# Groups of 384 tokens for the last two batches of the first product, and retimed start-up work, in a memory-attention kernel with two MLPs

## The chip, the core and the metric

The kernel runs on one core of a Trainium2 chip. The metric is the device time of one execution in microseconds. Three runs of the kernel before took 741.64 to 742.65 us, median 742.09. The engines are PE (TensorE, matmuls), PEld (its weight loads, which run beside matmuls), DVE (VectorE), ACT (ScalarE), POOL (GpSimd) and SP (SyncE, which here only issues DMAs).

## The reference

There are 4 batches, 8 heads, 576 tokens a batch, heads of 64 and 32 memory slots a head. `phi` gives a softmax over tokens, with which k and v are summed into 32 memory rows; q attends to these rows. The result, 2304 tokens of 512 features, goes through two MLPs of 512 x 2048 x 512, the first with a leaky ReLU, the second with the Mish function. All arithmetic is float32; the MLPs' weights come as 64-bit floats.

```python
a = exp(phi - max over tokens); a = a / (sum over tokens + 1e-9)
k_m = einsum('bhsm,bhsd->bhmd', a, k)
v_m = einsum('bhsm,bhsd->bhmd', a, v)
attn = softmax(q @ k_m.T / 8)               # over the 32 slots
x = (attn @ v_m), heads side by side        # 2304 x 512
h = x @ w_in;   x = max(0.01 * h, h) @ w_out
h = x @ w_in2;  out = (h * tanh(softplus(h))) @ w_out2
```

## The kernel before

**Numbers.** A float32 factor is split into a high part (a copy rounded to the matmul type fp32r) and a low part (the factor minus the high part). A product takes three matmuls: high weights by high data, low weights by high data, high weights by low data. `hi_lo` (L317) makes the two parts: the copy on ACT or DVE, the subtraction on DVE. The weights come as 64-bit floats and are decoded as two 32-bit words (`decode`, L359): ACT scales the high word (L369), the low word is shifted down to its top three bits on ACT (L374) or DVE (L376), DVE joins them (L411).

**Stage 1** is attention and the first MLP. The memory rows of v are multiplied into `w_in` first (`vw_tasks`, L955, matmuls of L975): for each batch and each chunk c of 512 of the 2048 hidden features there are two weight tiles `vw` (one for each group of four heads) of 2 x 512 words, high and low. There are eight buffers of that kind (`vw_tag`), taken in turn. `at` holds the attention weights, high and low, of 576 tokens; there are four such buffers, two a batch.

One item (`stage1`, L1215) is a block m of 128 hidden features for half a batch, 288 tokens. Its h product has 6 matmuls of 128x128 by 128x288 (L1226) into one of two PSUM tiles. ACT applies the leaky ReLU twice, into the high tile and into a plain one (L1240); DVE subtracts them into the low tile (L1247). Two items later (`LAG1`) come 8 matmuls of high parts and 4 of the low part with `w_out` (L1259) into four PSUM accumulators, one for each 128 output features. After the last block the accumulators are copied or added to `x1` (L1304 and L312). Batches 0 and 1 go in turns of one or two chunks while weights still arrive; batches 2 and 3 go through all 16 blocks, first for one half and then for the other.

**Stage 2** is the second MLP with Strassen's seven products at 384 columns (L1579, L1791; 256 columns at the end). Its data factors come from `split_x` (L1477), which needs the space of the attention buffers: all users of the pool `apool` must be through (`apool_users`, `keep`). Its weight factors (`split_w`, L1416) lie in the buffers that `w_out` and `vw` leave (`slots`, L1335). `w_in2` and `w_out2` are prepared during stage 1 (from L1113), partly in views of the attention's `kvq` buffers.

**Order.** Nothing waits by hand. Each piece of work is a task with a cost on each engine that can do it, a priority, tasks it depends on and buffers it takes. `Order.run` (L94) plays them through with those costs when the kernel is built: at each time an idle engine gets the ready task with the lowest priority, on the engine that would end it first, plus a bias (`TOP` for the low-word shift on DVE, `HI` for copies on DVE). A task that takes a buffer may start at most 8 items ahead. The order that comes out is fixed in the program of each engine; on the chip semaphores keep the dependences. Priorities count in items: `A1` and `A2` say how many items before a batch's first its attention is due, `S1` and `S2` how far apart its halves are, `WO` and `WC` how long before its item a block of w_out or a chunk of w_in is due, `V0` to `V2` the same for vw, `PL` and `BH` when and behind which chunk-1 loads of w_in the second batch's loads are issued on SP's queue, `HFD` the spacing of the steps of batch 0's attention, `XL` how long before the end of stage 1 the splits of x are due.

Of the kernel before, what the change touches and what calls it, by code (L numbers as in the profile page):

```python
# [23 lines left out]
def hop(a, b):  # L24
# [4 lines left out]


K = dict(
    LAG1=2, WIN=8, OB=2, RS=4, FILL=58, A1=10, S1=8.0,
    A2=30, S2=2.6, V1=2.4, V2=14, W2=45, W2S=3.8, O='phi0 kv0 phi1 q0 w0 kv1 q1 w1 w2 w3', HF0=-20.0, HF1=-7.0,
    HFD=0.3, TOP=0.1, HI=0.2, WO=2.0, WOL=1, WC=3.0, WC0=-38.0, V0=3.0, COLD=20, GL=1.5, AL=5.0, XL=22.0, T='0:1 0:1 1:2 0:2 1:2', SB=1,
    DW=280e3, DQ=1.3, DP=1.2, DS=0.78, DI=0.38, L4=0.5, L4P=1.6, L4S=0.8, L4T=5.0, MA=6, QL=4, PL=6, BH=(9,3,3,3,3), FK=-52.5, DWF=0.85, MV="......rvvrrvvrvr",
)


# [121 lines left out]
def kernel(  # L160
# [12 lines left out]
    nc = tc.nc  # L173
# [778 lines left out]

    win, win_ready, w_scr, w_loads = {}, {}, {}, [[] for _ in range(NC)]

    def vw_tasks(b, c, p0):  # L955
# [26 lines left out]

        t = keep(add(
            {"PE": 1.2}, p0, f, [x for g in range(NG) for x in vT[b, g][1] + win_ready[b, c, g]],
            pss + us, [vT[b, g][0] for g in range(NG)] + wbs,
        ))
        for g in range(NG):
            u, ps_b = us[g], pss[g]
            th, tl = hi_lo(
                p0 + 0.5 * g + 0.2, 512, lambda u=u: u.t[:, 0], lambda u=u: u.t[:, 1], lambda ps_b=ps_b: ps_b.t,  # L990
                [t], (), [u, ps_b], ps=True,
            )
            vw[b, c, g] = (u, th, tl)


# [12 lines left out]
    n1 = len(items)  # L1008
    at_item = {it: i for i, it in enumerate(items)}
    base = [at_item["1", b, 0, 0] for b in range(B)]  # L1010


    def wo_unit(m):
# [52 lines left out]
    def next_batch(b):  # L1066
        d, st = (K["A1"], K["S1"]) if b == 1 else (K["A2"], K["S2"])
        p = base[b] - d
        kv_rest(b, p, 0.08 * d / 2)
        score_rest(b, p + 0.1 * d, (p + 0.3 * d, p + 0.3 * d + st), 0.03 * d)  # L1070

    def next_vw(b, c):
        vw_tasks(b, c, at_item["1", b, 0, 4 * c] - (K["V1"] if b == 1 else K["V2"]))

    for b, cs in chunk_turns:
        if b and not cs[0]:
            next_batch(b)
        for c in cs:
            if b:
                next_vw(b, c)  # L1080
                continue
            w_chunk(c)
            for m in range(4 * c, 4 * c + 4):
                wo_unit(m)


    kv_again = [kvq.new([P, 2, 1024]) for _ in range(2)]
    opened = [add({"SP": 0.0}, K["W2"], lambda e, x=x: x.make(), (), [x]) for x in kv_again]

    class View:  # L1090

# [14 lines left out]
            b.make = make  # L1106
            return b

    views = [View(j) for j in range(3)]
# [102 lines left out]
    def passes(n):  # L1212
        return [(j, wi) for j in range(n) for wi in range(2)]

    def stage1(i, b, sub, m):  # L1215
        cols = slice(sub * NB1, (sub + 1) * NB1)
        c, j0 = m // 4, (m % 4) * P
        h = h_tag.new([P, NB1])
        us, ats = [vw[b, c, g] for g in range(NG)], [at[b, g] for g in range(NG)]

        def f1(e):
            h.make()
            n = 0
            for g in range(NG):
                for wi, ai in ((0, 0), (1, 0), (0, 1)):
                    nc.tensor.matmul(  # L1226
                        out=h.t, lhsT=us[g][0].t[:, wi, j0:j0 + P], rhs=ats[g][0].t[:, ai, cols],
                        start=(n == 0), stop=(n == 3 * NG - 1),
                    )
                    n += 1  # L1230

        t1 = add(
            {"PE": mm(NB1, 6)}, i, f1, [x for u in us for x in u[1:]] + [x for u in ats for x in u[1 + sub]], [h],
            [u[0] for u in us + ats],
        )
        t1.main = i
        eb, hb, lb = e_tag.new([P, NB1]), hi_tag.new([P, NB1], F32R), lo_tag.new([P, NB1], F32R)

        def lrelu(o):
            nc.scalar.activation(out=o, in_=h.t, func=AF.Prelu, alpha=0.01)  # L1240


        t4 = add({"ACT": act(NB1, True)}, i + 0.3, lambda e: lrelu(hb.make()), [t1], [hb], [h])
        t3 = add({"ACT": act(NB1, True)}, i + 0.4, lambda e: lrelu(eb.make()), [t1, t4], [eb], [h])
        t5 = add(
            {"DVE": dve(NB1)}, i + 0.6,
            lambda e: nc.vector.tensor_tensor(out=lb.make(), in0=eb.t, in1=hb.t.bitcast(F32), op=ALU.subtract),  # L1247
            [t4, t3], [lb], [eb, hb],
        )
        first, last = m in firsts(b), m + 1 in firsts(b) + [NM]  # L1250
        if first:
            for kk in range(NK):
                accs[kk] = acc_tag.new([P, NB1])
        ac = dict(accs)
        wu = wo[m]

# [11 lines left out]
        if first:  # L1268
            for kk in range(NK):
# [1 line left out]
                    ac[kk].make()  # L1271
                    mms([(kk, 0, 0), (kk, 1, 0)])

                hs.append(add({"PE": mm(NB1, 2)}, i + LAG1 + 0.01 * kk, f, [t4, *wu[1:], *hs[-1:]], [ac[kk]], [hb, wu[0]]))
        else:
            hs.append(
                add(
                    {"PE": mm(NB1, 2 * NK)}, i + LAG1, lambda e: mms([(kk, wi, 0) for kk, wi in passes(NK)]),
                    [t4, *wu[1:], *prev_l], (), [hb, wu[0], *ac.values()],
                )  # L1280
            )
# [1 line left out]
        if last:  # L1283
            for kk in range(NK):
                tl = add(
                    {"PE": mm(NB1)}, i + LAG1 + 0.1 + 0.01 * kk, lambda e, kk=kk: mms([(kk, 0, 1)]),
                    [t5, *hs], (), [lb, wu[0], ac[kk]],
                )
                key = (b, kk // 2)
                fresh = key not in x1  # L1290
                if fresh:
                    if b < B - 1:
                        x1[key] = [x1_tag.new([P, 2, S]), {}]
                    else:
                        x1[key] = [at_tag.new([P, 2, S]), {}]
                xb, evs = x1[key]
                add_in = (kk, sub) in evs

                def fe(e, kk=kk, xb=xb, fresh=fresh, add_in=add_in):
                    if fresh:  # L1300
                        xb.make()
                    o = xb.t[:, kk % 2, cols]
                    if add_in:
                        nc.vector.tensor_tensor(out=o, in0=ac[kk].t, in1=o, op=ALU.add)  # L1304
                    else:
                        copy(e, o, ac[kk].t)

                deps = [tl] + [x for x in list(evs.values())[:1]]
                if add_in:
                    deps.append(evs[kk, sub])  # L1310
                evs[kk, sub] = add(
                    {"DVE": dve(NB1)} if add_in else {"ACT": act(NB1, True), "DVE": dve(NB1)},
                    i + LAG1 + 0.2, fe, deps, [xb] if fresh else [], [ac[kk]] if fresh else [ac[kk], xb],
                )
        else:
            tl = add(
                {"PE": mm(NB1, NK)}, i + LAG1 + 0.1, lambda e: mms([(kk, 0, 1) for kk in range(NK)]),
                [t5, *hs], (), [lb, wu[0], *ac.values()],
            )
            prev_l.append(tl)  # L1320

    prev_l = []
    for i in range(n1):
        stage1(i, *items[i][1:])

# [566 lines left out]
```

## Time and profile before

| | us |
|---|---|
| median of 3 runs | 742.09 (741.64 to 742.65) |
| the profiled execution | 741.87 |
| its span, first to last instruction | 740.1 |
| PE busy in it | 731.0 |
| PEld busy | 701.3 |
| DVE busy | 550.6 |
| ACT busy | 402.5 |

The profile is of one execution. The span leaves out 1.8 us of the execution's own time. A busy PE is one with a matmul in flight; matmuls overlap, so the mean length of one (297 ns for 288 columns) is not the distance from one to the next. PEld's weight loads run beside the matmuls. The granted TensorE clock is 0.999 on the mean.

### The profile page before, as it was taken

To read this page: it belongs to the slowest core of one execution; us is meant where nothing else is said; L and a number is where in the kernel's file an instruction comes from. 1 tells how busy PE (TensorE), PEld (TensorE's weight loads), DVE (VectorE), ACT (ScalarE), POOL (GpSimd) and SP (SyncE) were. 2 spreads that over 40 slices of the span, in tenths; PEclk is the share of its full clock that TensorE was granted. 3 is DMA by queue.
4 is the path that set the end of the run, shared out by engine and by line. 5 is a ranking of instruction groups with operands and counts; after the bars stand their busy time and mean duration, and the time that the engine had idled before them with its cause. 6 is when DMAs were issued, how large, how long until landed. Compare 5 with 4: busy or idle time off the path is not lost.

```text
span 740.1 us, 15587 instructions
## 1 busy us (share of the span) xinstructions
PE 731.0 (99%) x5875; PEld 701.3 (95%) x5875; DVE 550.6 (74%) x1153; ACT 402.5 (54%) x877; POOL 0.7 (0%) x6
## 2 busy tenths in 40 slices
PE   8999999999999999999999999999999999999997
PEld 7788899888999989999999999999999999999997
DVE  6899868598766965647859797867777966775595
ACT  4866458565553775645546665544464644444442
POOL 0000000000000000000000000000000000000000
PEclk9999999999999999999999999999999999999999
DMA  9793957787869587863559898788988778996475
GB/s 353 299 318 115 350 172 232 229 274 229 290 207 286 171 274 269 262 233 101 199 199 338 302 312 254 233 271 249 300 278 264 250 239 258 297 290 207 126 218 182
DMA packets 99322, 183.73 MB, mean 248 GB/s; under 512 B 8112, under 2 KB 51376, under 8 KB 99248
## 3 DMA queue, kind: packets, MB, share of 16 engines
q1 hardware_dynamic: 99248, 182.75, 75.5%
q8 instruction: 46, 0.75, 0.4%
q14 instruction: 28, 0.23, 0.1%
HBM read 140.25 MB, written 42.47 MB: 247 GB/s over the span
## 4 chain that ended last, share of the span: by engine, by line
PE 96%; DVE 2%; ACT 1%; DMA 0%; issue 0%
PE acc_t L1259 28%; PE h_t L1579 22%; PE acc_t L1791 22%; PE h_t L1226 13%; PE misc_t L1791 2%; PE misc_t L975 2%; PE acc_t L1579 2%; PE acc_t L508 1%; PE misc_t L741 1%; PE misc_t L646 1%; DMA phi_t<-in_phi_dram 0%; PE h_t L865 0%; ACT raws_t L369 0%; ACT raws_t L374 0%; PE misc_t L689 0%
## 5 line engine op out<-in xcount | busy, mean ns | idle before, releaser
L1259 PE MATMUL acc_t<-hi_t,wo_t 128*128 128x288 f32 x1024 | 160.6, 297 | 0.4 <-DVE x_t L312 0.3
L1259 PEld LDWEIGHTS acc_t<-hi_t,wo_t 128*128 128x128 f32 x1024 | 142.9, 188 | 12.2 <-issue 7.0
L1226 PE MATMUL h_t<-at_t,vw_t 128*128 128x288 f32 x768 | 123.1, 296 | 0.0
L1791 PE MATMUL acc_t<-hi_t,wo_t 128*128 128x384 f32 x448 | 114.4, 336 | 0.0
L1240 ACT ACTIVATE hi_t<-h_t 128x288 fp32r<-128x288 f32 x128 | 52.6, 411 | 111.8 <-PE acc_t L1259 105.3
L1226 PEld LDWEIGHTS h_t<-at_t,vw_t 128*128 128x128 f32 x768 | 108.5, 188 | 0.7 <-issue 0.6
L1247 DVE TENSOR_TENSOR lo_t<-e_t,hi_t 128x288 fp32r<-128x288 f32 x128 | 57.3, 450 | 47.4 <-ACT e_t L1240 21.6
L1259 PE MATMUL acc_t<-lo_t,wo_t 128*128 128x288 f32 x512 | 89.8, 297 | 0.5 <-DVE lo_t L1247 0.5
L1791 PEld LDWEIGHTS acc_t<-hi_t,wo_t 128*128 128x128 f32 x448 | 81.3, 188 | 0.0
L1259 PEld LDWEIGHTS acc_t<-lo_t,wo_t 128*128 128x128 f32 x512 | 74.7, 188 | 6.3 <-issue 5.6
L1579 PE MATMUL h_t<-xt_t,vw_t 128*128 128x384 f32 x396 | 79.4, 336 | 0.0
L1579 PE MATMUL h_t<-xt_t,wo_t 128*128 128x384 f32 x352 | 75.8, 336 | 0.0
L1791 PE MATMUL acc_t<-lo_t,wo_t 128*128 128x384 f32 x224 | 75.6, 337 | 0.0
L1758 DVE TENSOR_TENSOR lo_t<-wo_t,hi_t 128x384 fp32r<-128x384 f32 x94 | 52.0, 554 | 31.4 <-ACT hi_t L310 29.9
L1579 PEld LDWEIGHTS h_t<-xt_t,vw_t 128*128 128x128 f32 x396 | 69.3, 188 | 0.0
L310 ACT ACTIVATE hi_t<-wo_t 128x384 fp32r<-128x384 f32 x78 | 40.7, 524 | 40.7 <-PE acc_t L1791 36.4
L1579 PEld LDWEIGHTS h_t<-xt_t,wo_t 128*128 128x128 f32 x352 | 61.9, 188 | 0.0
L1240 ACT ACTIVATE e_t<-h_t 128x288 f32<-128x288 f32 x128 | 52.0, 406 | 0.0
L1791 PE MATMUL acc_t<-wo_t,hi_t 128*128 128x256 f32 x240 | 45.0, 282 | 0.0
L1604 ACT ACTIVATE wo_t<-wo_t 128x384 f32<-128x384 f32 x53 | 27.6, 522 | 30.8 <-DVE wo_t L1598 30.6
L1791 PEld LDWEIGHTS acc_t<-lo_t,wo_t 128*128 128x128 f32 x224 | 42.0, 188 | 0.0
L310 ACT ACTIVATE wo_t<-h_t 128x384 f32<-128x384 f32 x50 | 24.5, 489 | 31.1 <-PE h_t L1579 31.1
(263 smaller groups left out, 1110.0 us busy)
## 6 DMA issues: line engine op xcount, KB each, us to landing
wo_t<-tscr SPq DMA_DIRECT2D x168, 256.0 KB, 3.8
vw_t<-wsum SPq DMA_DIRECT2D x32, 512.0 KB, 4.7
win_t<-wscr SPq DMA_DIRECT2D x24, 512.0 KB, 5.5
raw_t<-in_moe_w_in_dram SPq DMA_DIRECT2D x19, 512.0 KB, 7.5
raw_t<-in_moe_w_out_dram SPq DMA_DIRECT2D x17, 512.0 KB, 5.5
wsum<-vw_t SPq DMA_DIRECT2D x16, 512.0 KB, 4.5
wo_t<-wsum SPq DMA_DIRECT2D x16, 512.0 KB, 4.3
tscr<-raw_t SPq DMA_DIRECT2D x9, 512.0 KB, 5.5
```

What stands on the lines that cost most here:

```text
L310: nc.scalar.activation(out=o, in_=i, func=AF.Copy)
L508: nc.tensor.matmul(out=acc.t[rows, :].rearrange("p (j d) -> p j d", j=2), lhsT=phv()[rows, r, :], rhs=kv.t[rows, :2304].rearrange("p (j r ...
L646: nc.tensor.matmul(out=accs_[g].t[o:o + M, :].rearrange("p (j d) -> p j d", j=2), lhsT=ph.t[rows, x, j, :], rhs=kv[g].t[rows, :, x % 2, j, :],
L975: nc.tensor.matmul(out=pss[g].t[M * (h ^ g):M * (h ^ g) + M, :], lhsT=vT[b, g][0].t[rows, g, h ^ g if b else h // 2, :], rhs=wbs[g].t[rows ...
L1226: nc.tensor.matmul(out=h.t, lhsT=us[g][0].t[:, wi, j0:j0 + P], rhs=ats[g][0].t[:, ai, cols], start=(n == 0), stop=(n == 3 * NG - 1),)
L1240: nc.scalar.activation(out=o, in_=h.t, func=AF.Prelu, alpha=0.01)
L1247: lambda e: nc.vector.tensor_tensor(out=lb.make(), in0=eb.t, in1=hb.t.bitcast(F32), op=ALU.subtract),
L1259: nc.tensor.matmul(out=ac[kk].t, lhsT=wu[0].t[:, wi, kk * P:(kk + 1) * P], rhs=(hb if src == 0 else lb).t, start=(first and (wi, src) == ( ...
L1579: nc.tensor.matmul(out=h.t, lhsT=w[:, wi, c0:c0 + P], rhs=xp[b, xi].ap()[:, j], start=(first and j == 0 and k3 == 0), stop=(j == 1 and k3 ...
L1604: lambda e: nc.scalar.activation(out=t_of[x](), in_=h.t if h else t_of[x](), func=AF.Mish),
L1758: lambda e, hb=hb, lb=lb, src=src: nc.vector.tensor_tensor(out=lb.make(), in0=src(), in1=hb.t.bitcast(F32), op=ALU.subtract),
L1791: nc.tensor.matmul(out=ac[t].t, lhsT=T[:, wi, t * P:(t + 1) * P] if wide else x.t[:, t * P:(t + 1) * P], rhs=x.t if wide else T[:, wi], st ...
```

## The change

The tokens of batches 2 and 3, 1152 together, are cut into three groups of 384 rather than four of 288. The first lies in batch 2, the last in batch 3, and the middle one has 192 tokens of each. For the middle group a block's h is computed in two parts, side by side in one PSUM tile, each with the vw and at tiles of its own batch; ACT, DVE and the products with w_out treat the 384 columns as one, and the accumulators are copied out in two parts.

Batch 2's eight vw tiles are then in use until the middle group is through, so batch 3's tiles of chunk 0 lie elsewhere: one in the buffer of phi, the other in the two T buffers of attention (`Two`). Both are in `apool`, so the blocks that use them count among the users that `split_x` waits for. Positions of batches 2 and 3 count in steps of 384/288 items. The opening of the `kvq` views for w_in2 and w_out2 moves up into the loop over batches.

Eleven values change. Among them: the bias against the low-word shift on DVE rises from 0.1 to 0.4, the second batch's attention is due 12 items ahead rather than 10, w_out blocks are due at their item rather than two before it, and x is due 18 items before the end of stage 1 rather than 22.

```diff
-    ... A1=10, S1=8.0,
-    A2=30, S2=2.6, ...
-    HFD=0.3, TOP=0.1, HI=0.2, WO=2.0, WOL=1, WC=3.0, WC0=-38.0, V0=3.0, COLD=20, GL=1.5, AL=5.0, XL=22.0, ...
-    ... PL=6, BH=(9,3,3,3,3), ...
+    ... A1=12, S1=8.0,
+    A2=30, S2=3.5, ...
+    HFD=0.38, TOP=0.4, HI=0.2, WO=0.0, WOL=1, WC=3.5, WC0=-38.0, V0=2.0, COLD=20, GL=2.5, AL=5.0, XL=18.0, ...
+    ... PL=5, BH=(9,3,3,2,3), ...
...
+    class Two:
+        def __init__(self, bufs):
+            self.bufs = bufs
+        def make(self):
+            for x in self.bufs:
+                x.make()
+            self.t = self
+        def __getitem__(self, key):
+            return self.bufs[key[1]].t[key[:1] + key[2:]]
...
-            us.append(vw_tag.new([P, 2, 512], F32R))
+            if b == B - 1 and not c and g:
+                us.append(Two([T_tag.new([P, 512], F32R) for _ in range(2)]))
+            else:
+                us.append((vw_tag if b < B - 1 or c else tags["phi"]).new([P, 2, 512], F32R))
...
+            if b == B - 1 and not c:
+                keep(th), keep(tl)
...
-    items = [("1", b, sub, m) for b, m0, m1 in turns for sub in range(NSUB) for m in range(m0, m1)]
+    items = [("1", b, sub, m) for b, m0, m1 in turns for sub in range(NSUB) for m in range(m0, m1) if b < 2]
+    n_pair = len(items)
+    W3 = NB2 / NB1
+    for j in range(3):
+        parts = [(2, NB2 * j, min(NB2, S - NB2 * j))] if j < 2 else []
+        if j:
+            parts.append((3, 0 if j == 1 else S - NB2, NB2 if j == 2 else 2 * NB2 - S))
+        items += [("3", j, parts, m) for m in range(NM)]
...
-    def stage1(i, b, sub, m):
+    def stage1(i, step, parts, m):
+        N, b0 = sum(n for _, _, n in parts), parts[0][0]
...
-        h = h_tag.new([P, NB1])
+        h = h_tag.new([P, N])
...
+            o = 0
+            for x, (b, c0, n) in enumerate(parts):
+                for g in range(NG):
+                    for wi, ai in ((0, 0), (1, 0), (0, 1)):
+                        nc.tensor.matmul(
+                            out=h.t[:, o:o + n], lhsT=us[NG * x + g][0].t[:, wi, j0:j0 + P], rhs=ats[NG * x + g][0].t[:, ai, c0:c0 + n],
+                            start=((g, wi, ai) == (0, 0, 0)), stop=((g, ai) == (NG - 1, 1)), skip_group_check=True,
+                        )
+                o += n
...
+        if parts[-1][0] == B - 1 and not c:
+            keep(t1)
...
+        lag = LAG1 * step
...
-    slots = [
-        (base[B - 1] + NM + x, t) for x, _, t in sorted(
-            [(LAG1 + m, 0, wo_tag) for m in range(NM)] + [(4 * c + 3, 1, vw_tag) for c in range(NC) for _ in range(2)],
+    at_end = lambda m: n_pair + W3 * (2 * NM + m)
+    slots = [
+        (x, t) for x, _, t in sorted(
+            [(at_end(LAG1 + m), 0, wo_tag) for m in range(NM)] + [(at_end(4 * c + 3 if c else 0), 1, vw_tag) for c in range(NC) for _ in range(2)],
```

## Rows read from the trace of the kernel before

**Rows 1.** The page's parts 1 and 4: busy us of each engine; the chain that ended last.

```profile
PE 731.0 (99%) x5875; PEld 701.3 (95%) x5875; DVE 550.6 (74%) x1153; ACT 402.5 (54%) x877; POOL 0.7 (0%) x6
...
PE 96%; DVE 2%; ACT 1%; DMA 0%; issue 0%
```

**Rows 2.** Windows of one shape: stretch, length, busy and count by engine, clock, DMA.

```profile
350.00:370.00 20.00, 20.00 (x153) 20.00 (x153) 17.19 (x34) 11.66 (x27) 0.00 (x0) 1.00 0.52 184
480.00:520.00 40.00, 40.00 (x231) 40.00 (x230) 27.88 (x62) 17.36 (x35) 0.00 (x0) 1.00 0.83 256
...
710.00:730.00 20.00, 20.00 (x169) 20.00 (x168) 16.72 (x38) 9.78 (x19) 0.00 (x0) 1.00 0.81 247
```

**Rows 3.** Lines by shape: count, busy us, mean ns of one, idle before.

```profile
L1259 PE MATMUL acc_t<-hi_t,wo_t 128*128 128x288 f32 x1024 | 160.6, 297 | 0.4 <-DVE x_t L312 0.3
...
L1791 PE MATMUL acc_t<-hi_t,wo_t 128*128 128x384 f32 x448 | 114.4, 336 | 0.0
L1226 PEld LDWEIGHTS h_t<-at_t,vw_t 128*128 128x128 f32 x768 | 108.5, 188 | 0.7 <-issue 0.6
...
L1791 PE MATMUL acc_t<-wo_t,hi_t 128*128 128x256 f32 x240 | 45.0, 282 | 0.0
...
L623 PEld LDWEIGHTS misc_t<-ones,rm_t 128*128 128x128 f32 x12 | 1.6, 190 | 0.1
```

**Rows 4.** Timeline, weight loads near 56.6: start, us, instruction, count.

```profile
56.59 0.52 PEld L623 LDWEIGHTS misc_t<-ones,rm_t 128*128 128x128 f32 x4
```

**Rows 5.** Timeline, the boundary between batches 2 and 3.

```profile
307.53 0.30 PEld L1259 LDWEIGHTS acc_t<-hi_t,wo_t 128*128 128x128 f32 x2 [0.39 <-DVE x_t L312]
```

**Rows 6.** Timeline, the last vw preparation of batch 3.

```profile
298.13 1.09 PE L975 MATMUL misc_t<-win_t,vTb_t 64*32 64x512 f32 x16
...
299.96 1.22 DVE L1184 TENSOR_TENSOR kvq_t<-kvq_t 128x1024 fp32r<-128x1024 f32 x1
...
301.09 1.28 DVE L326 TENSOR_TENSOR vw_t<-misc_t,vw_t 128x512 fp32r<-128x512 f32 x2
```

**Rows 7.** Timeline, splits of x on DVE and stage 2's first product.

```profile
332.67 0.56 DVE L312 CAST xt_t<-x_t 128x768 fp32r<-128x768 f32 x1
...
349.68 0.56 DVE L1539 TENSOR_TENSOR raw_t<-raw_t,x_t 128x384 f32<-128x384 f32 x1
...
374.34 1.21 PE L1579 MATMUL h_t<-xt_t,wo_t 128*128 128x384 f32 x6
```

**Rows 8.** Windows of the end of stage 1.

```profile
330.00:350.00 20.00, 20.00 (x153) 20.00 (x152) 13.61 (x27) 10.94 (x27) 0.00 (x0) 1.00 0.31 107
350.00:374.00 24.00, 24.00 (x183) 24.00 (x183) 18.53 (x36) 13.16 (x32) 0.00 (x0) 1.00 0.59 208
```

**Rows 9.** Timeline, PE and DVE in the first items.

```profile
36.68 1.27 PE L1057 MATMUL acc_t<-ident 128*128 128x128 f32 x10
...
37.54 0.68 DVE L326 TENSOR_TENSOR wo_t<-raws_t,wo_t 128x512 fp32r<-128x512 f32 x1
...
39.01 0.79 PE L1259 MATMUL acc_t<-lo_t,wo_t 128*128 128x288 f32 x4 [0.47 <-DVE lo_t L1247]
```

**Rows 10.** Lines by shape from 0 to 110 us: low-word shifts.

```profile
L374 ACT ACTIVATE raw_t<-raw_t 128x512 int32<-128x512 uint16 x7 | 4.8, 691 | 0.0
...
L376 DVE TENSOR_SCALAR raw_t<-raw_t 128x512 int32<-128x512 int32 x5 | 2.1, 423 | 0.1
```

**Rows 11.** Windows, from 56 to 62 us.

```profile
56.00:62.00 6.00, 6.00 (x173) 5.56 (x172) 5.92 (x15) 4.61 (x12) 0.00 (x0) 1.00 0.71 244
```

**Rows 12.** Timeline, w_out block 4 and the second batch's first scores.

```profile
60.04 0.68 DVE L326 TENSOR_TENSOR wo_t<-raws_t,wo_t 128x512 fp32r<-128x512 f32 x1
...
61.78 1.32 PE L1259 MATMUL acc_t<-hi_t,wo_t 128*128 128x288 f32 x8
...
66.77 0.84 DVE L752 STREAM_TRANSPOSE T_t<-misc_t 128x288 f32<-128x288 f32 x2
...
75.42 0.81 DVE L326 TENSOR_TENSOR at_t<-T_t,at_t 128x288 fp32r<-128x288 f32 x2
```

More of the change, by code (lines that the diff above doesn't have):

```diff
@@ L953, with bufs_of @@
     win, win_ready, w_scr, w_loads = {}, {}, {}, [[] for _ in range(NC)]
+    class Two:
[7 more added lines that the diff above has]
+            return self.bufs[key[1]].t[key[:1] + key[2:]]
+    def bufs_of(us):
+        return [y for x in us for y in (x.bufs if isinstance(x, Two) else [x])]
     def vw_tasks(b, c, p0):
@@ L984, in vw_tasks @@
             {"PE": 1.2}, p0, f, [x for g in range(NG) for x in vT[b, g][1] + win_ready[b, c, g]],
-            pss + us, [vT[b, g][0] for g in range(NG)] + wbs,
+            pss + bufs_of(us), [vT[b, g][0] for g in range(NG)] + wbs,
         ))
@@ L1065 @@
         score_tasks(0, g, -59.5 + 10 * g, (-54.0, K["HF0"]) if not g else (-40.0, K["HF1"]), K["HFD"])
[L1066 to L1088, printed above, removed]
+    kv_again, opened = [], []
     class View:
@@ L1107, in new, with next_batch, next_vw @@
             return b
-    views = [View(j) for j in range(3)]
+    views = []
+    def next_batch(b):
+        d, st = (K["A1"], K["S1"]) if b == 1 else (K["A2"], K["S2"])
+        p = base[b] - d
+        kv_rest(b, p, 0.08 * d / 2)
+        score_rest(b, p + 0.1 * d, (p + 0.3 * d, p + 0.3 * d + st), 0.03 * d)
+    def next_vw(b, c):
+        vw_tasks(b, c, chunk_at(b, c) - (K["V1"] if b == 1 else K["V2"]))
+    for b, cs in chunk_turns:
+        if b and not cs[0]:
+            next_batch(b)
+            if b == B - 1:
+                kv_again += [kvq.new([P, 2, 1024]) for _ in range(2)]
+                opened += [add({"SP": 0.0}, K["W2"], lambda e, x=x: x.make(), (), [x]) for x in kv_again]
+                views += [View(j) for j in range(3)]
+        for c in cs:
+            if b:
+                next_vw(b, c)
+                continue
+            w_chunk(c)
+            for m in range(4 * c, 4 * c + 4):
+                wo_unit(m)
     more = Ring(raw.slots + rawm.slots[3:])
@@ L1232, in stage1 @@
+        halves = [[sub for sub in range(NSUB) if c0 < (sub + 1) * NB1 and c0 + n > sub * NB1] for _, c0, n in parts for g in range(NG)]
         t1 = add(
-            {"PE": mm(NB1, 6)}, i, f1, [x for u in us for x in u[1:]] + [x for u in ats for x in u[1 + sub]], [h],
-            [u[0] for u in us + ats],
+            {"PE": sum(mm(n, 6) for _, _, n in parts)}, i, f1,
+            [x for u in us for x in u[1:]] + [x for u, hs in zip(ats, halves) for sub in hs for x in u[1 + sub]], [h],
+            bufs_of([u[0] for u in us + ats]),
@@ L1245, in stage1 @@
+        t3 = add({"ACT": act(N, True)}, i + 0.4, lambda e: lrelu(eb.make()), [t1, t4], [eb], [h])
         t5 = add(
-            {"DVE": dve(NB1)}, i + 0.6,
+            {"DVE": dve(N)}, i + 0.6,
             lambda e: nc.vector.tensor_tensor(out=lb.make(), in0=eb.t, in1=hb.t.bitcast(F32), op=ALU.subtract),
@@ L1249, in stage1 @@
         )
-        first, last = m in firsts(b), m + 1 in firsts(b) + [NM]
+        lag = LAG1 * step
+        first, last = m in firsts(b0), m + 1 in firsts(b0) + [NM]
         if first:
             for kk in range(NK):
-                accs[kk] = acc_tag.new([P, NB1])
+                accs[kk] = acc_tag.new([P, N])
         ac = dict(accs)
@@ L1309, in stage1, with fe @@
[L1309 to L1314, printed above, removed]
+                o = 0
+                for b, c0, n in parts:
+                    key = (b, kk // 2)
+                    fresh = key not in x1
+                    if fresh:
+                        x1[key] = [x1_tag.new([P, 2, S]) if b < B - 1 else at_tag.new([P, 2, S]), {}]
+                    xb, evs = x1[key]
+                    add_in = (kk, c0) in evs
+                    def fe(e, kk=kk, xb=xb, fresh=fresh, add_in=add_in, o=o, c0=c0, n=n):
+                        if fresh:
+                            xb.make()
+                        src, x = ac[kk].t[:, o:o + n], xb.t[:, kk % 2, c0:c0 + n]
+                        if add_in:
+                            nc.vector.tensor_tensor(out=x, in0=src, in1=x, op=ALU.add)
+                        else:
+                            copy(e, x, src)
+                    deps = [tl] + [x for x in list(evs.values())[:1]]
+                    if add_in:
+                        deps.append(evs[kk, c0])
+                    evs[kk, c0] = add(
+                        {"DVE": dve(n)} if add_in else {"ACT": act(n, True), "DVE": dve(n)},
+                        i + lag + 0.2, fe, deps, [xb] if fresh else [], [ac[kk]] if fresh else [ac[kk], xb],
+                    )
+                    o += n
@@ L1322 @@
     prev_l = []
-    for i in range(n1):
-        stage1(i, *items[i][1:])
+    for i, (kind, x, y, m) in enumerate(items):
+        if kind == "1":
+            stage1(i, 1, [(x, y * NB1, NB1)], m)
+        else:
+            stage1(n_pair + W3 * (i - n_pair), W3, y, m)
+    at_end = lambda m: n_pair + W3 * (2 * NM + m)
     slots = [
-        (base[B - 1] + NM + x, t) for x, _, t in sorted(
-            [(LAG1 + m, 0, wo_tag) for m in range(NM)] + [(4 * c + 3, 1, vw_tag) for c in range(NC) for _ in range(2)],
+        (x, t) for x, _, t in sorted(
+            [(at_end(LAG1 + m), 0, wo_tag) for m in range(NM)] + [(at_end(4 * c + 3 if c else 0), 1, vw_tag) for c in range(NC) for _ in range(2)],
             key=lambda x: x[:2],
```

58 lines of the change are left out of this document (17 added, 41 removed).

## The prediction

> **What bounds the kernel now.** I read the engine busy times and the chain that ended last first [rows 1]. PE is busy 99% of the 740.1 us span and is 96% of the chain, so an edit counts only if it changes how many matmuls there are, how far apart they start, or how long PE waits between them. The busy time of PE cannot show the second, because matmuls overlap. I take it from stretches with one shape alone [rows 2]: a count takes in the matmuls that lie across the edges, so the spacing is (stretch + one mean length) / count. With the mean lengths of 0.297, 0.336 and 0.282 us [rows 3], 288 columns cost 20.297/153 = 132.7 ns, 384 columns 40.336/231 = 174.6 ns, 256 columns 20.282/169 = 120.0 ns. The granted clock is 1.00 in all three, its upper level (2.4 GHz).
>
> **The change part by part.** The profiled execution took 741.87 us (740.1 of span and 1.8 around it), 0.2 below the median of 742.09. The sum starts from 741.87.
>
> *The groups.* Two batches in four halves of 288 tokens are 4 x 16 blocks x 18 matmuls = 1152, at 132.7 ns 152.9 us. Three groups of 384 have 3 x 16 x 12 = 576 matmuls for w_out and, in the two groups that lie in one batch, 2 x 16 x 6 = 192 for h, all at 384 columns: 768 x 174.6 = 134.1 us. The middle group has half of its tokens in each batch, and each batch has its own weights, so its h needs 16 x 12 = 192 matmuls of 192 columns. The columns in total are the same; 192 instructions are gone. What a matmul of 192 columns costs decides the sign, and no row has one. From below: the line through 256 and 384 columns falls 0.427 ns a column and gives 92.7 ns, 17.8 us in all. From above: not dearer than 256 columns, 120.0 ns, 23.0 us. Nearest is a row that has the cost of a weight load bare: four loads of 128 x 128 for matmuls of a single column take 0.52 us [rows 4], with 190 ns for the last, so (520 - 190)/3 = 110 ns from one to the next although nothing streams behind them. The loads of stage 1 last the same (188 against 190 ns [rows 3]), so I take 110: 21.1 us. The sum is 134.1 + 21.1 - 152.9 = **+2.3 us** (from -1.0 to +4.2).
>
> The Trainium skill ("TensorE: Matmul & The Clock Gate", section "LDWEIGHTS (loading the stationary operand)") has the load at the number of its columns over 1.2, whatever the rows: 106.7 ns for 128. By that the 192 would cost 20.5 us and the groups +1.7. The 110 of the row agrees, and the rule speaks against the middle group: a stream of 192 columns is over before the next weights are in.
>
> *Boundaries.* Between halves PE waits for an accumulator to be copied out: weight loads stood 0.39 us [rows 5]. There is one boundary fewer: -0.4 (0 to -0.8). In the middle group the copies are two of 192 columns for each accumulator rather than one; they lie beside the next block's h.
>
> *Batch 3's weights.* The eight vw buffers now hold all of batch 2 until the middle group is through with each block of four. So vw(3,1) can start only when h of block 3 has been read, and h of block 4 waits for it; the same at blocks 8 and 12. That is a new wait, and behind it on PE stands all of stage 1. Before, the last of these preparations ran from its first matmul at 298.13 to the last lo at 302.37, 4.2 us, with one foreign DVE operation of 1.22 in between [rows 6]. What PE has meanwhile: the preparation's own 1.0, the lo products of block 1 (4 x 174.6 = 0.7), then hi and lo products of blocks 2 and 3 (2 x 2.1): 5.9 us. So I cost it at nothing; with two more DVE operations in front (1.22 each) it is 6.7 against 5.9, 0.8 three times, +2.4. Batch 3's first pair lies in the phi and T buffers, free when its attention is through, long before. Batch 3's attention is due 10.7 items sooner, since the middle group needs it: beside matmuls, on a DVE that is not full there, nothing.
>
> *The handover to stage 2.* The splits of x must now wait until the last group's first four blocks have used those apool buffers. They began at 332.67, and PE's first product of stage 2 was at 374.34 [rows 7]. Stage 1 ends near 390 in both, and a block of 384 takes 18 x 174.6 = 3.14 us, so the splits can begin near 390 - 12 x 3.14 = 352. The ten operations that stood before (first and last in rows 7, 5.7 us together) move to where DVE was busy 18.53 of 24 us, with 5.5 free, out of a stretch with 13.61 of 20 [rows 8]. It just fits, and on PE there is stage 1 work until 390 anyway. Zero, up to +2 if the first products come late. The wo slots fall free over 50 us instead of 38, which lets weight splits run sooner and cancels part of it. The third edit of that kind, opening the w2 views in the loop, keeps the order of the kvq buffers: nothing.
>
> *Start-up knobs.* In 36.68 to 39.01 PE runs fillers and then waits 0.47 for a lo on DVE, which has just split a w_out block [rows 9]. With w_out two items later those may stand behind the lo; but the next products need that w_out, so the work has to be done all the same. At most the filler and the wait go, -1.7; at worst the same again, +1.7; I take **-0.3**. The low-word shifts take 0.42 us on DVE and 0.69 on ACT [rows 10]; in the first 110 us only seven are on DVE (the five of that row and two more), so at most 3.0 us of DVE work move. The other values (V0, WC, PL, BH, HFD, S2) reorder the same instructions; PL and BH put the loads of batch 1, eight q transfers among them, further ahead on SP's queue, in front of w_out loads. GL is read nowhere, and A2 stays.
>
> *Second batch sooner, w_out later.* Between 56 and 62 us DVE is busy 5.92 of 6 [rows 11]. The lo of w_out block 4 starts at 60.04 and its products at 61.78, 1.1 us after it ends, while batch 1's scores follow from 66.77 to 76.2 [rows 12]. PE loses nothing to waits there now, so nothing is to be won; what can be lost is under the rivals. I take **+0.4**.
>
> Sum: 741.87 + 2.3 - 0.4 - 0.3 + 0.4 = **743.9 us**, 0.24% above the median. This kernel's measurements cannot tell less than 0.2% (1.5 us) from no change: under 740.6 is faster, over 743.6 slower.
>
> **The rivals.**
>
> *Columns alone (0.15).* The 192 pay 92.7 ns: 741.87 - 1.0 - 0.4 - 0.3 = 740.2 without a loss at start-up. For it: spacing follows the columns at 256, 288 and 384. Against it: the bare loads 110 apart. The Trainium skill has two rules that would bring this about: its section "Back-to-back issue gap" counts N/2.4 + 2.5, 82.5 ns for 192 columns, 15.8 us and -3.0 for the groups; and "Weight-path perf modes" has fast loads of 128 weights unless the type is FP32. Loads of 188 ns in stage 1 and 190 for plain FP32 show no such fast load here.
>
> *Start-up gains outweigh it (0.18).* Fillers and wait go (-1.7) and the first half of attention is done up to 1 us sooner, because DVE has the shifts no longer: 741.87 + 2.3 - 0.4 - 2.7 = 741.1, or 739.5 if three more such waits go. For it: DVE is the full engine before 80 us. Against it: before 39 us few shifts are on DVE.
>
> *w_out too late, slower (0.17).* One mechanism, at 56 to 80 us: batch 1's score chain of twelve DVE operations (the first and last in rows 12, 5.9 us in all) is put before the splits of w_out blocks 4 to 7. Their reserve is 1.1 us, so PE would wait 5.9 - 1.1 = 4.8 at most; half of it gives 743.9 + 2.4 = 746.3. It decides once more than two of these operations (0.75 each) stand in front. For it: the two edits push in the same direction on a full engine, and loads go the same way on SP. Against it: attention two items (2 x 18 x 132.7 = 4.8 us) sooner may be over before w_out has landed.
>
> *The edits don't bite (0.06).* Shifts stay where they are, the orders come out nearly alike, and gains of boundaries and start-up meet the weight loads: 742.0.
>
> **How the numbers follow.** My forecast has 0.44, its own range 742.4 to 745.2; 0.27 of it lies above 743.6. Faster: 0.10 of the first rival, 0.11 of the second, 0.21. Slower: 0.27 + 0.17 = 0.44. The rest is within 0.2%: 0.35. The range of 8 in 10 reaches from 739.8 (start-up gains with three waits, or columns alone) to 747.0 (w_out late by most of its price, or waits at batch 3's weights).
>
> **What would show it.** Right: h matmuls of 128x192 start 110 ns apart in the middle group, which is then 16 x (12 x 0.110 - 6 x 0.1746) = 4.4 us longer than the other two apart from inserted work; no waits for lo of vw in it; splits of x from about 350. Wrong: spacing of 93, first h well before 32 us, or waits on w_out or lo between 56 and 80.

## The result: slower by 0.95%, outside the predicted range

The changed kernel takes 749.41 us (median of 4 runs, 748.35 to 749.90), against 742.37 for the kernel before beside it (4 runs, 741.64 to 742.78). The ratio is 1.0095, interval 1.0080 to 1.0110: 7 us slower. The forecast was 743.9, with a range up to 747.0. The direction was given the largest chance (0.44), but neither the price nor the mechanism was among the cases. The profiled execution took 748.35 with a span of 746.5.

### The profile page after: what moved, and what is told of

The parts are those of the page before. It is cut to its first block, busy times and chain, and to the rows that moved or that the text cites. A ratio compares the mean times of both kernels' runs of the same rounds, so it can differ in the third digit from the quotient of the medians.

```text
span 746.5 us, 15120 instructions
## 1 busy us (share of the span) xinstructions
PE 734.5 (98%) x5683; PEld 704.6 (94%) x5683; DVE 550.9 (74%) x1137; ACT 400.2 (54%) x845; POOL 0.7 (0%) x6
## 4 chain that ended last, share of the span: by engine, by line
PE 97%; DVE 1%; issue 1%; DMA 0%; ACT 0%; DVEq 0%
PE acc_t L1300 27%; PE h_t L1624 22%; PE acc_t L1836 21%; PE h_t L1262 14%; PE misc_t L1836 2%; PE acc_t L1624 2%; PE misc_t L995 2%; PE acc_t L1087 1%; PE acc_t L508 1%; PE misc_t L646 1%; PE misc_t L741 1%; DMA phi_t<-in_phi_dram 0%; PE h_t L865 0%; PE misc_t L892 0%; PE misc_t L689 0%
## 5 line engine op out<-in xcount | busy, mean ns | idle before, releaser
L1300 PE MATMUL acc_t<-hi_t,wo_t 128*128 128x288 f32 (+1 forms) x896 | 157.0, 316 | 0.5 <-DVE x_t L312 0.4
L1300 PEld LDWEIGHTS acc_t<-hi_t,wo_t 128*128 128x128 f32 x896 | 138.7, 188 | 9.6 <-issue 5.0
L1280 ACT ACTIVATE hi_t<-h_t 128x288 fp32r<-128x288 f32 (+1 forms) x112 | 49.9, 446 | 126.5 <-PE acc_t L1300 116.4
L1262 PE MATMUL h_t<-at_t,vw_t 128*128 128x288 f32 (+2 forms) x720 | 117.0, 301 | 0.0
L1262 PEld LDWEIGHTS h_t<-at_t,vw_t 128*128 128x128 f32 x720 | 105.5, 190 | 0.2 <-issue 0.2
L1287 DVE TENSOR_TENSOR lo_t<-e_t,hi_t 128x288 fp32r<-128x288 f32 (+1 forms) x112 | 55.0, 495 | 53.8 <-PE acc_t L1300 30.9
L1624 PE MATMUL h_t<-xt_t,wo_t 128*128 128x384 f32 x424 | 89.8, 336 | 0.0
L1300 PE MATMUL acc_t<-lo_t,wo_t 128*128 128x288 f32 (+1 forms) x448 | 88.0, 318 | 0.0
L1300 PEld LDWEIGHTS acc_t<-lo_t,wo_t 128*128 128x128 f32 x448 | 71.1, 189 | 8.3 <-issue 7.5
L1624 PEld LDWEIGHTS h_t<-xt_t,wo_t 128*128 128x128 f32 x424 | 74.7, 188 | 0.0
L1624 PE MATMUL h_t<-xt_t,vw_t 128*128 128x384 f32 x324 | 65.4, 336 | 0.0
L1624 PEld LDWEIGHTS h_t<-xt_t,vw_t 128*128 128x128 f32 x324 | 56.9, 188 | 0.0
L1280 ACT ACTIVATE e_t<-h_t 128x288 f32<-128x288 f32 (+1 forms) x112 | 49.4, 441 | 0.0
```

The source lines that it names most:

```text
L1262: nc.tensor.matmul(out=h.t[:, o:o + n], lhsT=us[NG * x + g][0].t[:, wi, j0:j0 + P], rhs=ats[NG * x + g][0].t[:, ai, c0:c0 + n], start=((g, ...
L1300: nc.tensor.matmul(out=ac[kk].t, lhsT=wu[0].t[:, wi, kk * P:(kk + 1) * P], rhs=(hb if src == 0 else lb).t, start=(first and (wi, src) == ( ...
L1624: nc.tensor.matmul(out=h.t, lhsT=w[:, wi, c0:c0 + P], rhs=xp[b, xi].ap()[:, j], start=(first and j == 0 and k3 == 0), stop=(j == 1 and k3 ...
```

## The profile after

Parts 1 to 4 of the page, as in [rows 1], with the queue that brings the engines their programs:

```profile
PE 734.5 (98%) x5683; PEld 704.6 (94%) x5683; DVE 550.9 (74%) x1137; ACT 400.2 (54%) x845; POOL 0.7 (0%) x6
...
q8 instruction: 45, 0.74, 0.4%
...
PE 97%; DVE 1%; issue 1%; DMA 0%; ACT 0%; DVEq 0%
```

PE has 192 matmuls fewer, as counted. In the chain "issue" is up from 0% to 1% of the span: time in which PE waits for nothing that the profile shows. DVE and ACT have lost share in it. So the loss is not behind another engine. The view of PE's waits says where (who waited for what, us in total, times, longest us):

```profile
PE misc_t L646 <- issue: 3.1, 1, 3.1
...
PE acc_t L1300 <- DVE x_t L312: 0.4, 1, 0.4
```

L646 computes a batch's memory rows: 144 short matmuls (64 x 32 weights, 128 columns), each with a load, which come in one run for each batch from 1 to 3. The change does not touch that line. (Lines further down move: L1300 is the L1259 of before, L1262 its L1226.) The timeline of PE around batch 2's run, first after, then before (start, us, instruction, count, idle before):

```profile
124.49 2.21 PE L646 MATMUL misc_t<-kvq_t,phi_t 64*32 64x128 f32 x141
129.79 0.41 PE L646 MATMUL misc_t<-kvq_t,phi_t 64*32 64x128 f32 x3 [3.08 <-issue]
130.12 1.31 PE L1300 MATMUL acc_t<-hi_t,wo_t 128*128 128x288 f32 x6
```

```profile
136.61 2.25 PE L646 MATMUL misc_t<-kvq_t,phi_t 64*32 64x128 f32 x144
138.79 0.40 PE L1259 MATMUL acc_t<-hi_t,wo_t 128*128 128x288 f32 x1
```

Before, the run goes through in 2.25 us. After, PE stops behind 141 of the 144 matmuls, and the last three start 3.35 us after the one in front of them (3.08 us of that is idle time), although they read the same tiles as the others. Windows of PE alone over that place (stretch, length, busy and count, clock, DMA share, GB/s):

```profile
124.00:127.00 3.00, 2.71 (x146) 1.00 0.84 269
127.00:130.00 3.00, 0.21 (x3) 1.00 1.03 414
130.00:132.00 2.00, 2.00 (x13) 0.69 1.08 336
132.00:134.00 2.00, 2.00 (x10) 0.50 1.23 247
134.00:136.00 2.00, 2.00 (x23) 0.96 1.04 362
```

The wait costs twice. Behind it the granted clock falls from 1.00 (2.4 GHz) to 0.50 (1.2 GHz), and PE, busy all the time, is at 69, 50 and 96% of its clock in three windows of 2 us: 0.62 + 1.00 + 0.08 = 1.7 us by the clock alone. At half the clock matmuls of 288 columns start 240 ns apart here rather than 133, so I estimate the loss at 1.5 us.

In the wait, one packet of the program's queue arrives. Between 124 and 134 us the DMA view has a single packet of "q8 instruction", in this window of 1.1 us (packets, MB, share of 16 engines; 5.2% of 16 x 1.1 us is 0.9 us):

```profile
q8 instruction: 1, 0.02, 5.2%
```

The packet lasts from 127.48 to 128.40, and PE goes on at 129.79. Over the whole program 45 packets of 16 KB come for 2 x 5683 PE instructions, one for about 253. The run of 288 takes 2.2 us for more than one packet's worth; in the products of stage 1 as many instructions take some 17 us (253/2 x 132.7 ns).

Summed by the distance from each PE instruction to the next, the profiled executions differ by 6.5 us: L646 +3.4; h and w_out products together +3.6, of which some 1.5 is the clock; everything else -0.6.

The lines that answer to the prediction's other steps. A middle-group stretch with 192 columns, PE's timeline:

```profile
290.59 1.48 PE L1262 MATMUL h_t<-at_t,vw_t 128*128 128x192 f32 x12
291.90 1.59 PE L1300 MATMUL acc_t<-hi_t,wo_t 128*128 128x384 f32 x8
```

Twelve matmuls, 272 ns long each, span 1.48 us, (1.48 - 0.272)/11 = 110 ns apart. Batch 3's second pair of weights (answering [rows 6]), and stage 2's first product ([rows 7]):

```profile
282.55 1.09 PE L995 MATMUL misc_t<-win_t,vTb_t 64*32 64x512 f32 x16
...
284.98 0.61 PE L1300 MATMUL acc_t<-hi_t,wo_t 128*128 128x384 f32 x2 [0.45 <-DVE x_t L312]
285.43 0.81 PE L1262 MATMUL h_t<-at_t,vw_t 128*128 128x192 f32 x6
...
380.35 1.23 PE L1624 MATMUL h_t<-xt_t,vw_t 128*128 128x384 f32 x6
```

The wait at 284.98 is for an accumulator at the boundary into the middle group; none of the h products waits for vw. PE comes to stage 2's first product from stage 1's work, with no wait in front.

## The experiments

**Theory 1**: PE's program arrives in pieces, and where a piece falls due just ahead of a run of short instructions, PE eats what it has before the next piece is there. The eight start-up values put batch 2's run on such a place. **Rival 2**: those values are dear by the order that they give. **Rival 3**: the groups cost more than worked out. **Late data**: the last three matmuls wait for what they read. The expectations number the rivals by themselves: in the first four (groups only, values only, and the two with 72) rival 2 is the groups and rival 3 late data; the later ones say which rival they mean. The text keeps to the names above. All runs are beside the kernel before (742.0 to 742.5).

### One half of the change at a time

Groups only: the changed kernel with the eight start-up values of before (A1, HFD, TOP, WO, WC, V0, PL, BH).

```diff
-    A1=12 HFD=0.38 TOP=0.4 WO=0.0 WC=3.5 V0=2.0 PL=5 BH=(9,3,3,2,3)
+    A1=10 HFD=0.3 TOP=0.1 WO=2.0 WC=3.0 V0=3.0 PL=6 BH=(9,3,3,3,3)
```

> The groups of 384 with all start-up values as before (A1, HFD, TOP, WO, WC, V0, PL, BH); only XL and S2, which belong to the groups, are as in the change. Theory 1 (PE's program runs dry: 144 memory-row matmuls of batch 2, 288 instructions in 2.2 us, start just where the next 256 instructions have to be fetched): here these matmuls stand 176 instructions later, PE does not run dry, and the groups cost their 192 matmuls of 111 ns and little else: 744.5 to 745.5 us. Rival 2 (the groups themselves cost the time, through waits): 748 to 750 us. Rival 3 (late data for these matmuls): says nothing of the program's position; where the loads come as before, about 745.

Measured: 745.86, ratio 1.0047 (1.0035 to 1.0059), 0.4 above what theory 1 expected. Values only: the same diff the other way round, in the kernel before.

> The kernel before, with only the eight start-up values changed (A1, HFD, TOP, WO, WC, V0, PL, BH), no groups. The memory-row matmuls of batch 2 stand at the same place of PE's program as in the changed kernel. Theory 1: PE runs dry for about 3.3 us near 126 us, its clock then falls to half for some us (2.0 lost), and the start-up values win about 1 elsewhere: 746 to 747.5 us. Rival 2 (the groups cost the time): 741 to 742.5 us.

Measured: 747.70, ratio 1.0072 (1.0059 to 1.0084), 0.2 above theory 1's range, and in the timeline and the windows the same thing as in the changed kernel:

```profile
125.11 2.21 PE L646 MATMUL misc_t<-kvq_t,phi_t 64*32 64x128 f32 x141
130.45 0.63 PE L646 MATMUL misc_t<-kvq_t,phi_t 64*32 64x128 f32 x3 [3.12 <-issue]
```

```profile
128.00:132.00 4.00, 1.55 (x7) 0.68 1.03 407
132.00:136.00 4.00, 4.00 (x24) 0.50 1.16 267
```

So the 5.2 us belong to the values, not to the groups; rival 3 is left with 3.5 us (2.6 to 4.4) rather than 1.9. The two halves do not add up: 5.2 and 3.5 are 1.7 more than the 7.0 of the whole change.

### The same order, another place in the program

Six of the fillers ahead of stage 1 become four matmuls of one column each. In the trace a float32 matmul is two matmuls, each with a load, so 18 matmuls more are 72 PE instructions. The edit leaves the order of all others as it is, in the changed kernel and in the kernel with the values only.

```diff
+    spins = []
     def spin(e):
-        nc.tensor.matmul(out=..., lhsT=ident, rhs=ident, start=True, stop=True)
+        t, k = ..., 4 if 43 <= len(spins) < 49 else 1
+        for _ in range(k):
+            nc.tensor.matmul(out=t[:P if k == 1 else 32, :P if k == 1 else 1], lhsT=..., rhs=..., start=True, stop=True)
+        spins.append(0)
```

> The kernel before with the eight start-up values of the change and the 72 more PE instructions in the fillers, no groups. Theory 1: neither the dry program nor the 192-column matmuls: 740.5 to 742 us, possibly below the kernel before. Rival 3 (late data): as without the 72 instructions, 746 to 747.5. Rival 2: 741 to 742.5, both with and without them.

Measured: 742.35, ratio 1.0000 (0.9992 to 1.0009), 0.35 above theory 1's range. The run is whole:

```profile
125.92 2.25 PE L646 MATMUL misc_t<-kvq_t,phi_t 64*32 64x128 f32 x144
```

5.35 us are gone with 72 useless instructions more: rival 2 falls for this set of values, whose order by itself costs nothing. Late data falls with it, since nothing of the data's loads was edited.

> The changed kernel with 72 more PE instructions in the start-up fillers: six of the 58 filler matmuls become 24 of 32 weights by one column, of about the same total time, in a stretch where PE has nothing else; all other orders stay. Theory 1: the fetch now falls due 72 instructions ahead of the memory-row matmuls, some 5 us sooner, PE does not run dry and its clock stays: 743.5 to 745 us, no wait near 126 us. Rivals 2 and 3 (groups; late data): 749.4 us, the wait as before.

Measured: 745.17, ratio 1.0041 (1.0027 to 1.0056), 0.2 above theory 1's range. Batch 2's wait is gone, but batch 3's run now has one, with no fall of the clock behind it (timeline and windows):

```profile
194.76 2.03 PE L646 MATMUL misc_t<-kvq_t,phi_t 64*32 64x128 f32 x128
197.86 0.45 PE L646 MATMUL misc_t<-kvq_t,phi_t 64*32 64x128 f32 x16 [1.07 <-issue]
```

```profile
194.00:198.00 4.00, 2.93 (x145) 1.00 0.59 201
198.00:200.00 2.00, 2.00 (x29) 1.00 0.44 136
```

With 96 rather than 72 (the bound 51 for 49):

> The changed kernel with 96 added PE instructions ahead of stage 1 rather than the 72 of after_pad72 (745.17, a wait of 1.34 us in batch 3's L646 at 196.5). Theory 1: no piece of the program falls due just ahead of any of the three runs; no wait over 0.5 us in L646, time 743.5 to 744.5. Rival 2: as after_pad72, 745.2, with the wait at 196.5 still there. A rival by which any padding is as good as another: 745.2.

Measured: 745.75, ratio 1.0042 (1.0028 to 1.0057); a miss on the time. All three runs are whole, but just behind the padding the clock is down, as it is in the other kernel with 96 below (and not in after + 72). The windows:

```profile
32.00:34.00 2.00, 2.00 (x33) 0.99 0.93 173
34.00:36.00 2.00, 2.00 (x11) 0.50 0.52 110
36.00:38.00 2.00, 2.00 (x12) 0.65 0.86 288
```

So some 1.5 us are lost there (1.7 by the clock alone), where before all of them have 1.00. The only one of the five executions with a mean clock of 1.000 took 743.79, within the expected range; the other four (0.996 to 0.998) took 745.18 to 746.95. Padding with empty matmuls is not a clean remedy; why the clock fell stays open.

### Making the kernel before slow

If the place alone decides, the same 72 instructions must bring the wait into the kernel before.

> The kernel before, with six of its fillers (one 128x128 matmul each) replaced by four matmuls of one column each: 72 more PE instructions ahead of all of stage 1, nothing else. Theory 1 (PE's program comes in pieces, and a piece falls due just ahead of batch 2's run of 288 short instructions in L646): the 72 move that run to the place that it has in the changed kernel, so a wait of 2.5 to 3.5 us appears in L646 near 126 us, the granted clock falls to about 0.5 behind it, and the time is 746.5 to 749. Rival 2 (the eight values cost by the order they give): the order is untouched, 742.0 to 743.0 and no wait in L646. Either way the added matmuls themselves cost under 0.5 us, as in knobs_pad72.

Measured: 748.31, ratio 1.0075 (1.0062 to 1.0087). The wait is there:

```profile
140.05 2.22 PE L646 MATMUL misc_t<-kvq_t,phi_t 64*32 64x128 f32 x141
145.04 0.41 PE L646 MATMUL misc_t<-kvq_t,phi_t 64*32 64x128 f32 x3 [2.77 <-issue]
```

But it explains only 3.0 us (start to start): the clock behind it was 1.00, where theory 1 expected a fall, and the first h came at 35.8 rather than 32.3, behind a wait of 1.95 us ahead of the padding. So I ran the kernel a second time.

> The same kernel as before_pad72, to see a second profile. There the wait in L646 came (3.04 us) but the clock stayed at 1.00 behind it, and 3.5 us of the loss lay ahead of the first h, behind a wait of 1.95 us in L865 with a clock of 0.57 from 24 to 28 us; PE's instructions up to there are those of the kernel before. Theory 1 (the wait in L646 belongs to the place of the run; the start differs from run to run): again 2.8 to 3.5 us in L646; first h between 32.2 and 36; 745.5 if neither clock falls, up to 749. Rival 2: the wait in L646 was a chance of one run, and now it is under 0.5 us: 742.5 to 746.

Measured: 746.85, ratio 1.0062 (1.0046 to 1.0079), first h at 33.1. The wait came again, 3.50 us start to start, this time with a fall of the clock:

```profile
138.10 2.22 PE L646 MATMUL misc_t<-kvq_t,phi_t 64*32 64x128 f32 x141
143.55 0.64 PE L646 MATMUL misc_t<-kvq_t,phi_t 64*32 64x128 f32 x3 [3.23 <-issue]
```

```profile
140.00:143.00 3.00, 0.32 (x23) 1.00 1.04 334
143.00:146.00 3.00, 2.45 (x11) 0.57 1.01 157
```

The place does it in an order that has never had a wait there. Whether the clock falls behind a wait of this length differs between the two profiles.

### The places, counted

Counting PE's matmuls and loads in the order of the program, batch 2's run begins at instruction 2925 before and 2749 after. With about 253 a packet I take 256 as the period (an estimate) and list the remainder of each run's first instruction, with the longest wait within it (start to start, us):

| kernel | batch 1 | batch 2 | batch 3 |
|---|---|---|---|
| before | 93, none | 109, none | 225, none |
| after | 33, none | **189, 3.35** | 129, none |
| groups only | 93, none | 109, none | 165, 0.31 |
| values only | 33, none | **189, 3.39** | 253, none |
| values + 72 | 105, none | 5, none | 69, none |
| after + 72 | 105, none | 5, none | **201, 1.34** |
| after + 96 | 129, none | 29, none | 225, none |
| before + 72 | 165, none | **181, 3.04** | 41, none |
| after, WC and TOP back | 25, none | 121, none | 13, none |

Six of the 27 runs begin between 165 and 201; five of them have a wait, and none of the other 21 has.

The traces settle more than that. Count each trace's records of PE, with PE's semaphore instructions. Then all 19 waits of over 0.15 us for "issue" before a matmul, in the twelve profiles, stand where the records that went before are 193 more than a multiple of 256, and PE goes on 1.2 to 1.6 us after a packet of the instruction queue has landed. The waits of 3.35, 3.39, 3.04 and 3.50 us end 1.38, 1.30, 1.37 and 1.45 us after their packet, those of 1.34 and 0.31 us 1.35 and 1.39. So all of them are waits for PE's program, which theory 1 says, and 256 is the period. In this count the five runs with a wait begin at 162 to 193, where a run of 288 holds a whole 256 from one such place to the next, and none of the others begins between 136 and 216 (the sixth of the table, batch 1 of before + 72, is at 135).

How long PE stands depends on when the packet starts: in the four waits of 3 us it starts 0.6 to 1.2 us after the last matmul in front of the wait, in those of 1.34 and 0.31 us 1.1 and 2.4 us ahead of that matmul. In the windows that hold a wait of 3 us DMA's share is 0.82 to 1.04, in that of 1.34 it is 0.59. That busy DMA engines make the packet late would fit; no run tested it.

### Two remedies that took the wait away and not the time

Splitting the run into three tasks of 48 matmuls, with stage 1's products in between:

```diff
-        t7 = add({"PE": 2.2}, p0 + 3.8 * dp, fkv, [t5, *l_kv, t6], accs_, [ph, *kv])
+        for n, (j0, j1) in enumerate(((0, 3), (3, 6), (6, 9))):
+            t7 = [add({"PE": 0.8}, p0 + 3.8 * dp + 0.6 * n, lambda e, js=range(j0, j1): fkv(e, js), t7, ...)]
```

> The changed kernel without added instructions, but each batch's memory-row matmuls (L646) given to the planner as three tasks of 48 instead of one of 144, so that products of stage 1 stand between them. The first third of batch 2 stands at the same place in PE's program as the whole run did. Theory 1: PE no longer eats its program faster than it comes; the wait of 3.35 us shrinks to under 1 us, the clock stays at 1.00, time 743.8 to 745.5. Rival 2: order and place are the same, 748.5 to 750. A split that only moves the wait elsewhere would show it after the last third, near 130 us.

Measured: 750.45, ratio 1.0109 (1.0095 to 1.0122). The expectation failed on the time. The wait is down to 0.17 us (at the same place of the program), and the clock no longer falls:

```profile
124.00:130.00 6.00, 6.00 (x88) 1.00 0.67 202
130.00:136.00 6.00, 5.83 (x134) 1.00 1.01 406
```

But the planner, given other tasks, gave DVE another order. The largest new wait, at a boundary of stage 1, has a transposition of 1.37 us ahead of the accumulator's copies on DVE:

```profile
155.60 1.37 DVE L727 STREAM_TRANSPOSE kvq_t<-kvq_t 128x1152 f32<-128x1152 f32 x1
...
156.89 0.78 DVE L1348 TENSOR_TENSOR x_t<-acc_t,x_t 128x288 f32<-128x288 f32 x2
...
157.36 0.92 PE L1304 MATMUL acc_t<-hi_t,wo_t 128*128 128x288 f32 x5 [1.09 <-DVE x_t L1348]
```

In all, the distances of the w_out products sum to 213.4 us against 209.6 in after + 72: 3.8 us, where the medians differ by 5.3.

Putting two of the eight values back in the changed kernel (WC to 3.0, TOP to 0.1), which moves batch 2's run 188 instructions on:

> The changed kernel with two of its eight start-up values put back (WC 3.0, TOP 0.1), no added instructions. By the order of PE's instructions batch 2's run of L646 then begins 188 instructions later in the program than in the changed kernel (12 off its place in the kernel before) and batch 3's 140 later. Theory 1: no piece falls due within 40 instructions ahead of any of the three runs; no wait over 0.5 us in L646, clock 1.00 through 120 to 140 us; what is left is the groups' own price, 743.5 to 745.5. Rival 2 (the whole set of values is dear): six of eight are still there, 747 to 749.

Measured: 747.84, ratio 1.0078 (1.0064 to 1.0092), where theory 1 expected 743.5 to 745.5. The run is whole (136.95, 2.25 us, 144 matmuls, clock 1.00), but the h and w_out products take 319.4 us against 315.8 in after + 72. Seven of their distances are 0.27 to 0.59 us over the normal one, against two there, most of them at accumulators that had not yet been copied:

```profile
201.08 0.53 PE L1300 MATMUL acc_t<-hi_t,wo_t 128*128 128x288 f32 x2 [0.58 <-DVE x_t L1344]
...
282.88 0.62 PE L1300 MATMUL acc_t<-hi_t,wo_t 128*128 128x384 f32 x2 [0.42 <-DVE x_t L312]
```

So the numbers 747.84 and 750.45 are rival 2's, though its mechanism is not in the values: two new orders of the planner cost 2.7 and 5.3 us over after + 72, which comparisons of times alone would have laid on the values. The distances that stand out explain some 2 us more than in after + 72 in each; the rest was not followed up.

### What sets the price of 192 columns

After + 96, with 160 of the middle group's 192 h matmuls over 64 columns only, so that part of its h is left out:

```diff
+                        n1 = n if len(parts) < 2 or (g, wi, ai) == (0, 0, 0) else 64
-                            out=h.t[:, o:o + n], ... c0:c0 + n],
+                            out=h.t[:, o:o + n1], ... c0:c0 + n1],
```

> after_pad96 with 160 of the middle group's 192 matmuls of h streaming 64 columns instead of 192 (the first of each batch's six stays whole); h of the middle group is then partly left out. Load theory (a matmul there starts when its weight load of 128x128 is through): 110 to 112 ns apart as before, time within 0.6 us of after_pad96. Column theory (the line through 256 and 384 columns, 0.427 ns a column): 128 fewer columns are 55 ns each, 8 us less, about 736.

Measured: 745.08, ratio 1.0036 (1.0023 to 1.0049), against 745.75 for after + 96. Two thirds of the columns of ten in twelve matmuls are worth 0.06 us a block, first its timeline (twelve, then the next product), then that of after + 96:

```profile
289.09 1.42 PE L1263 MATMUL h_t<-at_t,vw_t 128*128 128x192 f32 x12
290.34 1.63 PE L1301 MATMUL acc_t<-hi_t,wo_t 128*128 128x384 f32 x8
```

```profile
287.43 1.48 PE L1262 MATMUL h_t<-at_t,vw_t 128*128 128x192 f32 x12
288.74 1.59 PE L1300 MATMUL acc_t<-hi_t,wo_t 128*128 128x384 f32 x8
```

1.25 against 1.31 us for twelve; by columns it would have been 0.55 less. (The medians differ by 0.67 us, a hair over the 0.6 expected; column theory was 8 us.) The columns do not set the distance, and a fixed price of a matmul does not either, since the 144 of L646 go through in 2.25 us with loads of 32 columns. What is left is the load of 128 columns, with the distance that bare loads have in [rows 4], 110 ns. The Trainium skill ("TensorE: Matmul & The Clock Gate", section "LDWEIGHTS (loading the stationary operand)") has a load at the number of its columns over 1.2, by which I estimate 106.7 ns for 128; 1.25/12 is 104 and 1.31/12 is 109, so the measurement agrees within 3 ns.

None of these kernels beats the kernel before; the values with 72 instructions equal it.

## Why the prediction was wrong, step by step

*What bounds the kernel*: right as far as it went. It named three ways in which an edit can count (how many matmuls, how far apart, how long PE waits between them) and then looked for waits only on tiles, loads and other engines. A fourth, PE's own program, was not in the list, though the waits of the kernel before have it as their largest entry, on a line after dense short matmuls (it is one of the 19; PE goes on 1.26 us after a packet there, and all twelve profiles have a wait of 0.4 to 2.0 us at that line):

```profile
PE h_t L865 <- issue: 1.4, 1, 1.4
```

*Start-up knobs*: **the step that failed.** It said that the other values "reorder the same instructions", took -0.3 and bounded it by 1.7 on either side. For the order itself that is right: values + 72 are 0.0 (-0.6 to +0.7) from before. But the same instructions at another place in the program cost 5.2 us (values only): 3.4 of wait for PE's program and a clock at half speed behind it. The prediction put that at nothing without a word on it, and no rival had the mechanism; the rival on the slower side was waits for w_out, worth 4.8 at most.

*The groups*: right in mechanism and near in size. The 192 matmuls are 110 to 111 ns apart, 21.1 us in all, as taken, and at the measured distances of the changed kernel the groups give +2.4 against the +2.3 forecast. Groups only came out 3.5 slower (2.6 to 4.4), 1.6 over the +1.9 with boundaries. In its trace 0.31 of that is a wait in batch 3's run, and h and w_out products together are 3.2 us longer than before; the rest is at the start (first h 33.0 against 32.3).

*Boundaries*: wrong by 0.7. Between the parts of batches 2 and 3 one wait for an accumulator stood before, 0.32 us over the normal distance [rows 5]; after, it is one of 0.61, that at 284.98. So +0.3 where -0.4 was forecast.

*Batch 3's weights* and *the handover*: right, no wait at either. The splits of x began at 341.7 rather than 332.7, most of them between 362 and 370; forecast was "about 350".

*Start-up in detail*: the wait of [rows 9] is gone and another of 0.51 stands at 52.7; first h at 32.16 against 32.33. Near the -0.3.

*Second batch sooner, w_out later*: no wait between 56 and 80 us [rows 11, 12]; the +0.4 and the rival "w_out too late" were not needed. The rival "columns alone" fell with the distance of 110 ns. The N/2.4 + 2.5 that it drew from the Trainium skill ("TensorE: Matmul & The Clock Gate", section "Back-to-back issue gap") is there the gap of a matmul without a budget for its load, which the section says is too little at small N; 110 against 82.5 bears that out. "Start-up gains" did not come.

The sum, put right for the profiled executions: +2.4 for groups, +0.3 for boundaries, +3.4 for the wait, some +1.5 for the clock: +7.6, where 741.87 to 748.35 is +6.5. The -1.1 between them is what is left over and was not measured by itself.

## What to carry to other kernels

Read the waits for "issue" on the engine that bounds the kernel, and ask of every run of short instructions how many there are against one packet of program. Here the runs are longer than a packet, so their cost depends on where they begin, and any edit ahead of it, even one off the path, moves them. When a reordering changes the time by some us, shift the same order by a few dozen instructions before you blame or praise the order. A fix that goes through a planner is a new order as well: look at what else has moved before the time is read.

## What was not expected of the hardware

- PE can stop for its own program: 3.0 to 3.5 us start to start four times (3.35, 3.39, 3.04 and 3.50), each time behind 141 of 144 matmuls, with a packet of the instruction queue inside the wait and PE going on 1.30 to 1.45 us after it.
- Behind the waits of 3.35, 3.39 and 3.50 us the granted clock fell to 0.50, and behind those of 1.34 and 3.04 it stayed at 1.00; with the clock, values only lost 5.2 us to a wait of 3.4.
- 72 more instructions made one kernel 5.4 us faster and another 4.8 to 5.8 slower, of which 0.8 to 3.5 came ahead of its first h.
